# Attention for one query over a long cache: the wait for the output's landing moves behind the block's closing barrier

## The chip, the cores and the metric

The kernel runs on one core of a Trainium2 chip. The metric is the device time of one execution in microseconds; three runs of the kernel before gave 632.2, 632.3 and 632.31 us, median 632.3.

A core has five engines, each with its own instruction queue: TensorE (PE; its weight loads are listed as PEld), VectorE (DVE), ScalarE (ACT), GpSimd (POOL) and SyncE (SP). SyncE computes nothing here; it issues transfers, which sixteen DMA engines carry out. Engines and transfers wait for one another through semaphores: a transfer adds 16 to its semaphore when it has landed.

## The reference

The computation is attention with grouped queries: 32 query heads, 8 heads of K and V, one query position, 65,536 cached positions, 128 elements per head. Inputs and output are bf16.

```
B, Hq, Hkv, Sq, Sk, D = 1, 32, 8, 1, 65536, 128
k, v = repeat each head of k and v Hq // Hkv = 4 times
scores = einsum("bhqd,bhkd->bhqk", q, k) * D ** -0.5
p      = softmax(scores, axis=-1)
out    = einsum("bhqk,bhkd->bhqd", p, v)
```

K and V together are 268.4 MB and each byte is used once; the output is 8 KB.

## The kernel before

Each head's 65,536 positions are four chunks of 16,384, and two chunks make a pair, so there are 16 pairs. SyncE's function `sync_engine` issues all loads: for each pair two K transfers into `kbuf[0]` and `kbuf[1]` (4 MB each; cut into smaller pieces for the first and last pair) and V into `vbuf`. Before it reloads a buffer it waits for `kfree` or `vfree`, which the engines raise when they have read it.

For every chunk TensorE transposes K in tiles of 128 (line 116), VectorE and ScalarE copy the transposed tiles from PSUM to SBUF (lines 174 and 171), TensorE multiplies them with four queries (line 125), VectorE and GpSimd find the running maximum, ScalarE takes the exponentials and their sums, and TensorE multiplies with V (line 137). VectorE rescales and adds up the partial results. At the end of a head it divides by the sum (line 248, into `oT`).

Behind the loops stands a short tail, in which each step waits for the one before:

- `tensor_engine` waits for the last head (`t_o`) and transposes the result back (line 162).
- `vector_engine` rounds it to bf16 into `orow` (line 276) and raises `t_row`.
- `sync_engine` waits for `t_row`, issues the 8 KB output transfer (line 361), and waits for its landing on `o_sem` (line 362).

The five functions are the parts of one block (`nc.Block()`). Closing the block, which before happens in `es.close()` on line 370, sends every engine by a branch into a common closing barrier: each engine but GpSimd reports with a DRAIN that raises one semaphore, GpSimd waits for four reports and raises a second semaphore by four, and each of the others takes its release from it. All of these carry line 370 in the trace of before. A wait that stands directly ahead of an instruction is carried by it: before, SyncE's wait on `o_sem` is carried by SyncE's branch out of the block. A similar barrier opens the program (line 383).

`es.close()` then gives the semaphores and buffers back, which adds no instruction.

Of the kernel before, what the change touches and what calls it, by code (L numbers as in the profile page):

```python
# [29 lines left out]
def starts(sizes):  # L30
    return [sum(sizes[:i]) for i in range(len(sizes))]
# [8 lines left out]
def bass_standalone__gqa_softmax__decode_kernel(nc, q, k, v, out):  # L40
# [11 lines left out]
    S = es.enter_context  # L52
# [4 lines left out]
    def sem(name):  # L57
        return S(nc.semaphore(name))
# [43 lines left out]
    q_sem, o_sem, s_x, t_if, t_id, t_o, t_row = (  # L102
        sem(n) for n in ("q_sem", "o_sem", "s_x", "t_if", "t_id", "t_o", "t_row"))
# [219 lines left out]
    def sync_engine(e):  # L323
        W = T * D

        def src(x, p):
            h, c = p // 2, p % 2
            return x[h, c * 2 * P * T:(c + 1) * 2 * P * T, :].rearrange("(p t) d -> p (t d)", p=P)

        def pieces(to, s, sizes, sems):  # L330
            for a, w, sm in zip(starts(sizes), sizes, sems):
                e.dma_start(to[:, a * D:(a + w) * D], s[:, a * D:(a + w) * D]).then_inc(sm, 16)

        def tokens(sems):
            for sm in sems:
                e.sem_inc(sm, 16)

        for p in range(NP):
            ks, vs = src(kf, p), src(vf, p)
            for n in range(2):  # L340
                if p:
                    e.wait_ge(kfree[n], p)
                if p in (0, NP - 1):
                    pieces(kbuf[n], ks[:, n * W:(n + 1) * W], K_PIECES[n], kp[n])
                else:
                    e.dma_start(kbuf[n][:, :], ks[:, n * W:(n + 1) * W]).then_inc(kp[n][0], 16)
                    tokens(kp[n][1:])
            if p:
                e.wait_ge(vfree, p)
            if p in (0, NP - 2):  # L350
                for n in range(2):
                    e.dma_start(vbuf[:, n * W:(n + 1) * W], vs[:, n * W:(n + 1) * W]).then_inc(vp[n][0], 16)
                tokens(vp[1][1:])
            elif p < NP - 1:
                e.dma_start(vbuf[:, :], vs).then_inc(vp[0][0], 16)
                tokens(vp[1])
            else:
                for n in range(2):
                    pieces(vbuf[:, n * W:(n + 1) * W], vs[:, n * W:(n + 1) * W], V_PIECES[n], vp[n])
        e.wait_ge(t_row, 1)  # L360
        e.dma_start(of, orow[:, :]).then_inc(o_sem, 16)
        e.wait_ge(o_sem, 16)

    block = S(nc.Block())
    block.tensor(tensor_engine)
    block.vector(vector_engine)
    block.scalar(scalar_engine)
    block.gpsimd(gpsimd_engine)
    block.sync(sync_engine)
    es.close()  # L370

# [26 lines left out]
```

## Time and profile before

| | |
|---|---|
| median of three runs | 632.3 us (632.2 to 632.31) |
| profiled execution, its own time | 632.31 us |
| its span, first to last instruction | 630.5 us |
| time of that execution outside the span | 1.81 us |
| mean granted TensorE clock | 0.77 of full speed |
| moved | 268.59 MB, 426 GB/s over the span |

The span runs from the first to the last instruction of the program on any engine; the execution's own time is longer by what lies around it. In the views, a name with a q behind it (SPq, POOLq) is the engine's sequencer, which handles branches, semaphores, DRAINs and the issue of transfers; these aren't counted as busy time. "Us to landing" is the time from a transfer's issue to its semaphore. A row of a waits view names who waited, for whom, the total in us, how often and the longest. A row of the view of one line gives durations in ns (least, median, greatest) and the first and last start in us.

### The profile page before, as it was taken

To read this page: it belongs to the slowest core of one execution; us is meant where nothing else is said; L and a number is where in the kernel's file an instruction comes from. 1 tells how busy PE (TensorE), PEld (TensorE's weight loads), DVE (VectorE), ACT (ScalarE), POOL (GpSimd) and SP (SyncE) were. 2 spreads that over 40 slices of the span, in tenths; PEclk is the share of its full clock that TensorE was granted. 3 is DMA by queue.
4 is the path that set the end of the run, shared out by engine and by line. 5 is a ranking of instruction groups with operands and counts; after the bars stand their busy time and mean duration, and the time that the engine had idled before them with its cause. 6 is when DMAs were issued, how large, how long until landed. Compare 5 with 4: busy or idle time off the path is not lost. (4 is left out here: it accounts for less than half of the span.)

```text
span 630.5 us, 27839 instructions
## 1 busy us (share of the span) xinstructions
PE 485.2 (77%) x12290; PEld 479.9 (76%) x12290; DVE 316.8 (50%) x691; ACT 184.4 (29%) x411; POOL 16.0 (3%) x46
## 2 busy tenths in 40 slices
PE   6766859688696877958679585894968949689895
PEld 6766859687696877958679585894958849689894
DVE  5523717347173472825628165381644707447382
ACT  2321413314143140412504124041341413414241
POOL 0000000000000000000000000000000000000000
PEclk9877959779597795967959687595876958769595
DMA  8999999999999999999999999999999999999996
GB/s 357 438 429 446 437 412 453 412 453 424 420 445 420 445 422 431 453 414 451 414 432 447 418 447 418 432 451 414 451 414 451 428 418 447 420 430 432 417 436 260
DMA packets 9034, 268.59 MB, mean 426 GB/s; under 512 B 1088, under 2 KB 1088, under 8 KB 1856
## 3 DMA queue, kind: packets, MB, share of 16 engines
q1 hardware_dynamic: 8976, 268.45, 99.0%
q8 instruction: 6, 0.10, 0.1%
q14 instruction: 4, 0.03, 0.0%
q10 hardware_dynamic: 48, 0.01, 0.0%
HBM read 268.44 MB, written 0.01 MB: 426 GB/s over the span
## 5 line engine op out<-in xcount | busy, mean ns | idle before, releaser
L116 PE MATMUL trb<-ident,kbuf 128*128 128x128 bf16 x4096 | 335.9, 233 | 39.6 <-PEq L37 39.3
L174 DVE COPY ktb<-trb 128x1024 bf16<-128x1024 bf16 x384 | 255.1, 691 | 115.8 <-DVEq L37 115.0
L116 PEld LDWEIGHTS trb<-ident,kbuf 128*128 128x128 bf16 x4096 | 262.6, 104 | 41.0 <-issue 41.0
L171 ACT ACTIVATE ktb<-trb 128x1024 bf16<-128x1024 bf16 x128 | 131.1, 1024 | 386.5 <-ACTq L37 386.5
L125 PE MATMUL qkb<-qcur,ktb 128*128 128x4 bf16 x4096 | 175.2, 165 | 12.5 <-PEq L37 8.9
L137 PE MATMUL pvb<-pts,vbuf 128*128 128x4 bf16 x4096 | 112.3, 166 | 86.8 <-PEq L37 80.3
L137 PEld LDWEIGHTS pvb<-pts,vbuf 128*128 128x128 bf16 x4096 | 111.0, 104 | 88.1 <-issue 88.0
L125 PEld LDWEIGHTS qkb<-qcur,ktb 128*128 128x128 bf16 x4096 | 157.1, 97 | 14.8 <-issue 13.6
L286 ACT ACTIVATE pts<-qkb,negm 128x128 bf16<-128x128 f32 x128 | 50.7, 546 | 0.0
L212 DVE TENSOR_TENSOR acc<-acc,pvb 128x4 f32<-128x4 f32 x24 | 3.8, 158 | 85.3 <-DVEq L37 85.3
L286 ACT ACTIVATION_READ_ACCUMULATOR pts<-qkb,negm 128x1 f32 x128 | 35.4, 276 | 0.0
L183 DVE TENSOR_REDUCE cmax<-qkb 128x4 f32<-128x512 f32 x32 | 21.9, 686 | 21.5 <-DVEq L37 21.5
L210 DVE COPY acc<-pvb 128x4 f32<-128x4 f32 x8 | 1.3, 163 | 49.8 <-DVEq L37 49.8
L318 POOL PARTITION_ALL_REDUCE cmaxa<-cmax x32 | 11.9, 371 | 533.0 <-POOLq L37 533.0
L282 ACT ACTIVATE alpha<-dm 128x4 f32<-128x4 f32 x24 | 4.9, 202 | 46.2 <-ACTq L37 46.2
L193 DVE TENSOR_TENSOR m<-m,cmaxa 128x4 f32<-128x4 f32 x24 | 3.9, 163 | 8.0 <-DVEq L37 7.8
L202 DVE TENSOR_TENSOR acc<-acc,alpha 128x4 f32<-128x4 f32 x24 | 3.9, 163 | 6.6 <-DVEq L37 6.6
L203 DVE TENSOR_TENSOR lp<-lp,alpha 128x4 f32<-128x4 f32 x24 | 3.9, 163 | 3.7 <-DVEq L37 0.4
L204 DVE TENSOR_TENSOR lp<-lp,rsum 128x4 f32<-128x4 f32 x24 | 3.9, 163 | 3.5
L194 DVE TENSOR_TENSOR dm<-m 128x4 f32<-128x4 f32 x24 | 3.9, 162 | 3.5
L320 POOL PARTITION_ALL_REDUCE la<-lp x8 | 3.4, 430 | 72.7 <-POOLq L37 72.7
L195 DVE TENSOR_SCALAR negm<-m 128x4 f32<-128x4 f32 x24 | 3.9, 162 | 0.0
(32 smaller groups left out, 20.5 us busy)
## 6 DMA issues: line engine op xcount, KB each, us to landing
kbuf<-in_k_dram SPq DMA_DIRECT2D x28, 4096.0 KB, 26.7
vbuf<-in_v_dram SPq DMA_DIRECT2D x5, 4096.0 KB, 30.7
kbuf<-in_k_dram SPq DMA_DIRECT2D x6, 2048.0 KB, 21.6
kbuf<-in_k_dram SPq DMA_DIRECT2D x4, 512.0 KB, 11.9
kbuf<-in_k_dram SPq DMA_DIRECT2D x2, 1024.0 KB, 14.3
vbuf<-in_v_dram SPq DMA_DIRECT2D x1, 2048.0 KB, 29.6
vbuf<-in_v_dram SPq DMA_DIRECT2D x1, 1024.0 KB, 31.7
vbuf<-in_v_dram SPq DMA_DIRECT2D x2, 512.0 KB, 32.8
```

What stands on the lines that cost most here:

```text
L116: ins = pe.transpose(trb[j % NTB][:, i * P:(i + 1) * P], kv[:, t, :], ident[:, :])
L125: ins = pe.matmul(qkb[n][:, t * R:(t + 1) * R], lhsT=ktb[:, off:off + P], rhs=qcur[:, :], start=True, stop=True)
L137: ins = pe.matmul(pvb[n][:, 0:R], lhsT=vv[:, t, :], rhs=pts[n][:, t * R:(t + 1) * R], start=t == 0, stop=t == T - 1)
L171: e.activation(dst, trb[j % NTB][:, :], AF.Copy).then_inc(eva, 1)
L174: e.tensor_copy(dst, trb[j % NTB][:, :]).then_inc(evd, 1)
L183: e.tensor_reduce(cmax[:, :], qkb[n][:, :].rearrange("p (t g) -> p g t", g=R), AX.X, ALU.max).then_inc(cm, 1)
L193: own(e, e.tensor_tensor(mn[:, :], mo[:, :], cmaxa[:, :], ALU.max), xd)
L194: e.tensor_tensor(dm[:, :], mo[:, :], mn[:, :], ALU.subtract)
L195: e.tensor_scalar(negm[:, :], mn[:, :], -scale, None, ALU.mult).then_inc(ng, 1)
L282: e.activation(alpha[:, :], dm[:, :], AF.Exp, scale=scale)
L286: ins = e.activation(pv[:, g, :], sv[:, g, :], AF.Exp, bias=negm[:, g:g + 1], scale=scale, accum_out=rsum[:, g:g + 1])
L318: e.partition_all_reduce(cmaxa[:, :], cmax[:, :], P, bass.bass_isa.ReduceOp.max).then_inc(cma, 1)
```

## The change

The block is closed explicitly, and SyncE's wait on `o_sem` is issued behind it. SyncE now issues the output transfer, goes through the closing barrier with the other engines, and then waits for the transfer. The instructions of the other four engines stay the same and in the same order. On SyncE the branch no longer carries a wait, and one semaphore instruction is added as its last.

```
         e.wait_ge(t_row, 1)
         e.dma_start(of, orow[:, :]).then_inc(o_sem, 16)
-        e.wait_ge(o_sem, 16)
-
-    block = S(nc.Block())
-    block.tensor(tensor_engine)
-    block.vector(vector_engine)
-    block.scalar(scalar_engine)
-    block.gpsimd(gpsimd_engine)
-    block.sync(sync_engine)
+
+    with nc.Block() as block:
+        block.tensor(tensor_engine)
+        block.vector(vector_engine)
+        block.scalar(scalar_engine)
+        block.gpsimd(gpsimd_engine)
+        block.sync(sync_engine)
+    nc.sync.wait_ge(o_sem, 16)
     es.close()
```

## The prediction

> **What bounds the kernel now.** I began with the page's head and its strip of forty slices, to see which resource is full, and then cut the span at the points where the last stage changes its nature.
>
> ```profile
> span 630.5 us, 27839 instructions
> ...
> PE 485.2 (77%) x12290; PEld 479.9 (76%) x12290; DVE 316.8 (50%) x691; ACT 184.4 (29%) x411; POOL 16.0 (3%) x46
> ...
> DMA  8999999999999999999999999999999999999996
> ```
>
> ```profile
> core 0: us, PE busy (x) PEld busy (x) DVE busy (x) ACT busy (x) POOL busy (x), PEclk, DMA share, GB/s
> 0.72:626.50 625.78, 484.25 (x12273) 479.25 (x12273) 316.20 (x688) 184.42 (x411) 15.84 (x42) 0.77 1.00 429
> 626.50:628.71 2.21, 0.94 (x17) 0.61 (x17) 0.60 (x3) 0.00 (x0) 0.00 (x0) 0.50 0.00 0
> 628.71:630.11 1.40, 0.00 (x0) 0.00 (x0) 0.00 (x0) 0.00 (x0) 0.00 (x0) 0.50 0.03 6
> 630.11:630.50 0.39, 0.00 (x0) 0.00 (x0) 0.00 (x0) 0.00 (x0) 0.00 (x0) 0.50 0.00 0
> ```
>
> The page says that no engine is full (77% at most) and that the transfer engines are busy in nine tenths or more of nearly every slice. The table by windows sharpens it: for the first 626.5 us the DMA share is 1.00 at 429 GB/s. So the kernel is bound by loading K and V, and whatever sits beside that stream is free. Then come three short stages with no load in flight. The first, 2.21 us, finishes the arithmetic. The second, 1.40 us, has no engine busy and a DMA share of 0.03. The third, 0.39 us, has nothing busy at all. Only the last two can be touched by the change, so I read the timeline there, and then SyncE's own waits.
>
> ```profile
> 627.38 0.16 DVE L212 TENSOR_TENSOR acc<-acc,pvb 128x4 f32<-128x4 f32 x1 [4.29 <-DVEq L37]
> 627.69 0.16 DVE L248 TENSOR_TENSOR oT<-acc,recip 128x4 f32<-128x4 f32 x1
> 627.96 0.10 PEld L162 LDWEIGHTS qkb<-identf,oT 128*32 128x32 f32 x1 [0.82 <-issue]
> 627.99 0.37 PE L162 MATMUL qkb<-identf,oT 128*32 128x128 f32 x1 [0.76 <-DVE oT L248]
> 628.40 0.28 DVE L276 CAST orow<-qkb 32x128 bf16<-32x128 f32 x1 [0.56 <-PE qkb L162]
> 628.71 0.36 SPq L361 DMA_DIRECT2D out_dram<-orow  x1
> ```
>
> ```profile
> SPq L361 <- DVE orow L276: 34.9, 1, 34.9
> ...
> SPq L370 <- DMA out_dram<-orow: 1.0, 1, 1.0
> ...
> SPq L370 <- PEq L370: 0.2, 1, 0.2
> ```
>
> ```profile
> qsb<-in_q_dram ACTq DMA_DIRECT2D x1, 8.0 KB, 2.8
> out_dram<-orow SPq DMA_DIRECT2D x1, 8.0 KB, 1.4
> ```
>
> The timeline is a strict sequence: last sum, division, transposition back, rounding, and the issue of the output transfer at 628.71. SyncE has been waiting for that rounding for 34.9 us. The list of transfers gives 1.4 us from issue to landing: 628.71 + 1.4 = 630.1, and the waits agree, since SyncE's issue ends at 628.71 + 0.36 = 629.07 and it then waits 1.0 us for the landing. What follows the landing is in the view of line 370, where the block closes; the columns are engine queue, instruction, durations in ns, first and last start in us.
>
> ```profile
> L370 POOLq EVENT_SEMAPHORE  x2: 17/17/17, 630.3 to 630.4; - x2
> L370 ACTq DRAIN  x1: 8/8/8, 619.5 to 619.5; - x1
> L370 POOLq DRAIN  x1: 403/403/403, 622.3 to 622.3; - x1
> L370 PEldq DRAIN  x1: 415/415/415, 628.0 to 628.0; - x1
> L370 DVEq DRAIN  x1: 318/318/318, 628.4 to 628.4; - x1
> L370 SPq COMPARE_BRANCH  x1: 38/38/38, 630.1 to 630.1; - x1
> L370 SPq DRAIN  x1: 7/7/7, 630.3 to 630.3; - x1
> L370 SPq EVENT_SEMAPHORE  x1: 17/17/17, 630.4 to 630.4; - x1
> L370 ACTq EVENT_SEMAPHORE  x1: 17/17/17, 630.4 to 630.4; - x1
> L370 DVEq EVENT_SEMAPHORE  x1: 21/21/21, 630.4 to 630.4; - x1
> L370 PEldq EVENT_SEMAPHORE  x1: 51/51/51, 630.4 to 630.4; - x1
> ```
>
> This is the closing barrier. Each engine reports in with a DRAIN, GpSimd collects the reports and releases everyone with two semaphore instructions, and each engine takes its release. ACT has been there since 619.5, GpSimd since 622.3 + 0.4, the last of the others, DVE, since 628.4 + 0.3 = 628.7. SyncE alone is late: its branch out of the block carries the wait for the landing, runs at 630.1, reports at 630.3, and all are released at 630.4. The last instruction of the program is the release of TensorE, which ends the span at 630.5.
>
> **The change, part by part.** Nothing before 628.71 is touched: the loops, the loads and their semaphores are the same instructions in the same order on every engine. Two things differ on SyncE.
>
> First, the wait leaves the branch at the block's end. SyncE's branch can then run when the issue of the output is done, at 629.07, and no longer at 630.1. Behind the branch lie, by the rows of line 370, 0.2 us to SyncE's report, 0.1 us to GpSimd's release and 0.1 us until the last engine has taken it: 630.5 − 630.1 = 0.4 us, and by the window that runs from the landing to the end 0.39 us. In the new order this stretch runs from 629.07 to 629.5. The other engines are no obstacle, since the last of them reported at 628.7. So the whole barrier lies under the transfer, with 630.1 − 629.5 = 0.6 us to spare. The cover is the 1.0 us that remains of the flight after the issue; a transfer that landed 0.6 us sooner would still hide it, one that landed 1.0 us sooner would leave the 0.4 us bare, as now.
>
> What could make SyncE reach the barrier later than 629.07 is its own issue. Its length here is 0.36 us; the loads of line 332 bound it.
>
> ```profile
> L332 SPq DMA_DIRECT2D kbuf<-in_k_dram x12: 328/426/502, 0.7 to 580.4; - x12
> L332 SPq DMA_DIRECT2D vbuf<-in_v_dram x5: 327/432/438, 591.6 to 593.4; - x5
> ```
>
> At 502 ns it would be 0.14 us later, which the 0.6 us absorbs.
>
> Second, a wait for the landing is added behind the barrier, as an instruction of its own on SyncE. Before, it rode on the branch. Nothing is queued behind it on SyncE and no engine waits for SyncE after the barrier. Its price is its own execution after the landing: the semaphore instruction of SyncE in the rows above takes 17 ns, 0.02 us. Its bounds are that 0.02 us below and, above, the 0.2 us that passed between the branch's wake-up at 630.1 and SyncE's next instruction at 630.3, in case what delays that one is the wake-up and not the branch. I take the lower end, because the instruction is of the very kind of the 17 ns row, while the 0.2 us stand behind a branch.
>
> The sum: the end of the span moves from 630.5 to the landing plus the wait, 630.11 + 0.02 = 630.13; that is 0.37 us less. Around the span lie 632.31 − 630.5 = 1.81 us in the profiled execution, which no row of the trace resolves. I leave them as they are for the likeliest case, so 632.31 − 0.37 = 631.94 us. The profiled execution, 632.31, is that of the runs to 0.01 us (median 632.3), so the forecast is 631.9. That is 0.06% of the time. A difference within 0.2%, that is 1.26 us, is about what a measurement of this kernel can tell from no change; so I call this no change, with a small gain inside it.
>
> **The rivals.**
>
> The barrier isn't hidden, so that the change doesn't do what it says. The rows of line 370 speak for it in one way: a DRAIN does wait for its engine's unfinished work (415 ns on TensorE behind the transposition of 0.37 us, 318 ns on VectorE behind the rounding of 0.28 us, against 8 ns on ScalarE, which was idle). SyncE's DRAIN is 7 ns, but its transfer had landed by then, so no row shows a DRAIN of SyncE with a transfer in flight. If it waited for the landing, only the branch and its 0.2 us would go under the transfer: report at 630.1, release and taking of it 0.2 us, end at 630.3 and 632.1 in all. Against it: the DMA instruction itself ends on SyncE after 0.36 us, 1.0 us before landing, so for the engine's queue the work is done by then. If the unresolved 1.81 us are what counts and not SyncE's end, it stays at 632.3.
>
> The early release gains more than the barrier. Four engines are free at 629.5 in place of 630.5. If their work after the program is what fills the 1.81 us, it starts 1.0 us sooner: 629.5 + 1.81 = 631.3 us. It speaks for this that 1.81 us is a good deal of time for nothing; against it, that something must wait for SyncE, and SyncE is done only at 630.13, leaving 1.2 us for its part. This case is bounded by 1.0 us, 0.16%, and doesn't leave the band. The Trainium skill, on the page "Runtime: NRT & Kernel Launch", in the section "The ~15µs preamble/postamble breakdown", states that a barrier of about 1.5 us follows the kernel and waits for all engines, and elsewhere in the section that such a barrier walks the engines at 44 ns for each of 8 hops. By it the engines released early would wait there for SyncE and this rival could win at most the hops already walked, an estimate of 0.35 us, thus 631.6 in place of 631.3; no row here shows that part, and the page's sum of stages is larger than the 1.81 us that this case has outside the span.
>
> The landing becomes late, which is the way to a slower kernel. The four released engines do whatever they do after the program (the 1.81 us) while the output is still in flight, from 629.5 to 630.1; before, the transfer was alone, with a DMA share of 0.03. The list of transfers shows what the same 8 KB cost under traffic: the queries, issued at the start beside the first loads, took 2.8 us against 1.4. At that price the landing is at 631.5 and the time 631.94 + 1.4 = 633.3. It decides against the change from 0.37 us of delay on, and passes 0.2% from 0.37 + 1.26 = 1.63 us. Against it: the queries met several 512 KB loads, and nothing like that is issued behind the program in this trace; the window after the landing shows 0 GB/s. The skill's page "DMA: Bandwidth & Descriptors", section "Latency and other measured facts", puts the access to HBM at 0.2 us on average and 2 us at high load and makes it the larger part of a transfer's fixed cost. By that figure the rival would cost up to 1.8 us, an estimate, and give 633.7; by the trace, where the bus is empty at this place, the low end holds.
>
> **How the numbers follow.** Barrier hidden, outside unchanged, 631.9: 0.76. Barrier not hidden, 632.1 to 632.3: 0.10. Early release gains more, 631.3 to 631.9: 0.07. Late landing, 632.3 to 633.7: 0.04, of which half passes 0.2%. That leaves 0.03 for what no row shows, a load stream of 626 us that runs slightly differently in a newly built program, equally to both sides. The first three cases span 631.3 to 632.3; the runs before lie within 0.11 us (632.2 to 632.31), and some part of the late landing belongs into eight tenths, so the range is 631.2 to 632.7. Faster by over 0.2% needs 1.26 us, more than the 1.0 us of the second rival: 0.03, from the load stream and from an early release that saves more than the rows allow. Slower by over 0.2%: 0.04, half of the late landing and the load stream. Within: 0.93.
>
> **What would show it.** In the profile after, the view of the block's closing line should have SyncE's branch at about 629.1 and all releases at about 629.5, before the landing; a semaphore wait of SyncE alone should stand at 630.1 and be the last instruction; the span should be 630.1, and the first 626.5 us should be the same in DMA share and rate. A SyncE DRAIN of about 1 us instead of 7 ns would show the first rival; a time outside the span of clearly less than 1.81 us the second; a landing of over 1.8 us the third. The prediction is wrong if the load stage moves by a microsecond, or if the time outside the span grows by what the span loses.

## The result and the profile after

Twenty runs of the changed kernel gave 631.31 to 631.57 us, median 631.4; twenty of the kernel before, 632.13 to 632.43, median 632.3. The two sets don't overlap. The ratio is 0.9986, with a 95% interval of 0.998 to 0.9992: 0.9 us faster, 0.14%, inside the prediction's band of 0.2%. The forecast was 631.9, so the kernel gained 0.9 us where 0.4 us was predicted.

First the windows of the profile after, cut at the same places as before: at 0.72 and 626.50 us, at the issue of the output transfer, here 628.73, and at its landing.

```profile
0.72:626.50 625.78, 483.85 (x12273) 478.82 (x12273) 316.08 (x688) 184.44 (x411) 15.88 (x42) 0.77 1.00 429
626.50:628.73 2.23, 0.94 (x17) 0.61 (x17) 0.60 (x3) 0.00 (x0) 0.00 (x0) 0.50 0.00 0
628.73:630.11 1.38, 0.00 (x0) 0.00 (x0) 0.00 (x0) 0.00 (x0) 0.00 (x0) 0.50 0.03 6
```

The load stage has the same DMA share, 1.00, and the same 429 GB/s; the arithmetic tail is 2.23 us against 2.21. Nothing came from there. Next the line on which the block now closes, 363, and SyncE's wait behind it, line 369.

```profile
L363 POOLq EVENT_SEMAPHORE  x2: 17/17/17, 629.3 to 629.4; - x2
L363 ACTq DRAIN  x1: 8/8/8, 619.2 to 619.2; - x1
L363 POOLq DRAIN  x1: 404/404/404, 622.3 to 622.3; - x1
L363 PEldq DRAIN  x1: 415/415/415, 628.0 to 628.0; - x1
L363 DVEq DRAIN  x1: 318/318/318, 628.4 to 628.4; - x1
L363 SPq DRAIN  x1: 118/118/118, 629.1 to 629.1; - x1
L363 SPq EVENT_SEMAPHORE  x1: 17/17/17, 629.4 to 629.4; - x1
...
L363 PEldq EVENT_SEMAPHORE  x1: 51/51/51, 629.4 to 629.4; - x1
```

```profile
L369 SPq EVENT_SEMAPHORE  x1: 17/17/17, 630.1 to 630.1; - x1
```

```profile
SPq L369 <- DMA out_dram<-orow: 0.7, 1, 0.7
```

SyncE's DRAIN, its report to the barrier, starts at 629.1, everyone is released at 629.4, and SyncE alone is left: its waits show 0.7 us on the landing, until 630.1. The list of transfers still gives the output 1.4 us to landing. The span is 630.1 us against 630.5. So the part that the trace shows has the size that was forecast. The rest of the gain isn't in the trace: in the profiled executions the time outside the span is 631.48 − 630.1 = 1.4 us after, against 1.8 us before. Over the runs, each with its own span (given to 0.1 us), the mean outside is 1.33 us after (20 runs) and 1.81 us before (108 runs taken beside the experiments, in four groups of 1.80 to 1.81). The experiments ask where those 0.48 us went.

### The profile page after: what moved, and what is told of

Same layout as the page of the kernel before. It is cut to its first block, busy times and chain, and to the rows that moved or that the text cites. A ratio compares the mean times of both kernels' runs of the same rounds, so it can differ in the third digit from the quotient of the medians.

```text
span 630.1 us, 27839 instructions
## 1 busy us (share of the span) xinstructions
PE 484.8 (77%) x12290; PEld 479.4 (76%) x12290; DVE 316.7 (50%) x691; ACT 184.4 (29%) x411; POOL 16.1 (3%) x46
```

## The experiments

Every kernel of the experiments was run eleven times, beside runs of the kernel before, whose median lay between 632.25 and 632.30. The row of the changed kernel has the twenty runs from above; it wasn't run again beside the experiments. "Outside" is the mean over the runs of time less span. A ratio's interval is about 0.09% to either side, some 0.6 us, so what is compared below are medians and the ranges of the runs, which are a few tenths of a microsecond wide.

| kernel | median (range), us | ratio to before (95%) | outside, us |
|---|---|---|---|
| changed kernel (SyncE waits) | 631.40 (631.31–631.57) | 0.9986 (0.998–0.9992) | 1.33 |
| wait inside again | 632.29 (632.17–632.34) | 1.0 (0.9991–1.0009) | 1.80 |
| all five wait | 631.92 (631.78–632.16) | 0.9995 (0.9986–1.0004) | 1.82 |
| VectorE waits | 631.50 (631.45–631.68) | 0.9987 (0.9978–0.9996) | 1.45 |
| ScalarE waits | 631.54 (631.50–631.68) | 0.9989 (0.998–0.9998) | 1.47 |
| TensorE waits | 631.72 (631.59–631.93) | 0.9992 (0.9983–1.0001) | 1.62 |
| GpSimd waits | 631.94 (631.86–632.30) | 0.9995 (0.9986–1.0004) | 1.86 |
| all but SyncE wait | 632.02 (631.83–632.10) | 0.9996 (0.9987–1.0005) | 1.84 |
| SyncE sends and waits twice | 632.81 (632.70–632.91) | 1.0008 (0.9999–1.0017) | 1.31 |
| GpSimd later, 1 clear | 631.51 (631.41–631.61) | 0.9987 (0.9978–0.9996) | 1.40 |
| GpSimd later, 2 clears | 631.76 (631.64–631.87) | 0.9992 (0.9983–1.0001) | 1.64 |
| GpSimd later, 3 clears | 632.03 (631.89–632.14) | 0.9995 (0.9986–1.0004) | 1.90 |
| GpSimd later, 6 clears | 632.77 (632.73–632.94) | 1.0008 (0.9999–1.0017) | 1.90 |

### The place of the wait, or the new form of closing

My theory after the result was the prediction's second rival: four engines are released 1.0 us earlier, and work of theirs after the program, which no view shows, used to set the end. The rival was that a newly laid out program merely has another overhead. Two runs separate them. The first keeps the new form and puts the wait back.

```
         e.dma_start(of, orow[:, :]).then_inc(o_sem, 16)
+        e.wait_ge(o_sem, 16)
...
-    nc.sync.wait_ge(o_sem, 16)
```

> The block is closed explicitly as in the changed kernel, but SyncE's wait for the landing stands inside the block again, ahead of the barrier. It tells the place of the wait from the new form of closing the block. Theory A (what was gained comes from the order of landing and barrier: 0.4 us of barrier, and about 0.45 us outside the span because four engines are released early): this is the kernel before, 632.3 us, span 630.5, 1.8 us outside. Rival D (the 0.45 us outside the span come from the newly laid out program and not from the release): 631.8 to 631.9, span 630.5, 1.35 us outside.

Measured: 632.29 us, 1.80 us outside, as the kernel before. Its closing line shows the old order, with SyncE's branch at the landing and the report behind it.

```profile
L364 SPq COMPARE_BRANCH  x1: 38/38/38, 630.1 to 630.1; - x1
L364 SPq DRAIN  x1: 7/7/7, 630.3 to 630.3; - x1
```

The form alone is worth nothing. The second keeps the barrier hidden but lets nobody go early.

```
-    nc.sync.wait_ge(o_sem, 16)
+    for e in (nc.tensor, nc.vector, nc.scalar, nc.gpsimd, nc.sync):
+        e.wait_ge(o_sem, 16)
```

> Behind the closing barrier all five engines wait for the landing, not SyncE alone. The barrier stays hidden, but no engine is released early. Theory A: the span is that of the changed kernel, 630.1 us, but the time outside it goes back to 1.8 us, so 631.9, which was the forecast for the changed kernel. Rival D: 631.4 as the changed kernel, 1.35 us outside the span.

Measured: 631.92 us, 1.82 us outside. The view of the added line shows all five leaving together.

```profile
L370 SPq EVENT_SEMAPHORE  x1: 17/17/17, 630.0 to 630.0; - x1
L370 ACTq EVENT_SEMAPHORE  x1: 17/17/17, 630.0 to 630.0; - x1
L370 POOLq EVENT_SEMAPHORE  x1: 17/17/17, 630.0 to 630.0; - x1
L370 DVEq EVENT_SEMAPHORE  x1: 21/21/21, 630.0 to 630.0; - x1
L370 PEldq EVENT_SEMAPHORE  x1: 51/51/51, 630.0 to 630.0; - x1
```

This splits the gain: hiding the barrier is worth 632.3 − 631.92 = 0.4 us, and the early release of the others 631.92 − 631.40 = 0.5 us. The span is that of the changed kernel, 630.1 us, in both; the half microsecond lies wholly outside it.

### Which engine sets the end

Call an engine's closing part what has to be added to its last instruction to reach the end of the execution; any time that lies ahead of the first instruction is in this number, alike for every engine. Three forms of the theory were open: closing parts that run side by side (A1), a chain that walks the engines in order (A2), or parts that hinder one another when all start together (A3). In each of four runs another engine is the one that waits.

```
-    nc.sync.wait_ge(o_sem, 16)
+    nc.scalar.wait_ge(o_sem, 16)      # or nc.tensor, nc.vector, nc.gpsimd
```

> Behind the barrier ScalarE waits for the landing in place of SyncE; the other four are released at about 629.5. It asks how long each engine's own work after the program is. Theory A1 (each engine has a closing part of its own, they run side by side, and the time is that of the last; SyncE's is 1.35 us, and one other engine's is 1.8): 631.4 or less, unless ScalarE is the engine with 1.8 us, then 631.9. Theory A2 (the closing work is one chain that walks the engines in order, and an engine that comes late leaves only the steps behind it): a time between 631.1 and 632.0 that depends on ScalarE's place in the chain. Theory A3 (the closing parts hinder one another when all five start at once): 631.4, whichever engine it is.

> Behind the barrier TensorE waits for the landing in place of SyncE. Theory A1 (parallel closing parts): 631.4 or less, or 631.9 if TensorE is the engine whose part takes 1.8 us; its semaphore instruction is also the slowest, 51 ns against 17. Theory A2 (a chain in order): another time than with ScalarE, the two differing by the steps between them. Theory A3 (parts that hinder one another): 631.4 as with any engine.

> Behind the barrier VectorE waits for the landing in place of SyncE. So far the time outside the span is 1.34 us with SyncE last, 1.47 with ScalarE, 1.60 with TensorE and 1.83 with all five. Theory A1 (closing parts side by side, the longest sets the end): then VectorE or GpSimd has a part of 1.8 us, and with VectorE last the time is 631.9 if it is VectorE, under 631.9 if it is GpSimd. Theory A2 (a chain, each later engine cheaper): 1.2 to 1.75 us outside, below the 1.83 of all five, with VectorE as with GpSimd.

> Behind the barrier GpSimd waits for the landing in place of SyncE. Theory A1: 631.9 (1.8 us outside) if VectorE last stayed clearly below that, since one engine must have the 1.8 us. Theory A2: below 1.75 us outside here too, so that no single engine has the 1.83 us and the engines' closing parts add to one another.

Measured outside the span: VectorE 1.45, ScalarE 1.47, TensorE 1.62, GpSimd 1.86 us, beside SyncE's 1.33. The view of GpSimd's added wait has it at the landing, inside a span of 630.1 us:

```profile
L369 POOLq EVENT_SEMAPHORE  x1: 17/17/17, 630.0 to 630.0; - x1
```

The engines differ, so A3 falls. GpSimd alone costs as much as all five together (1.82), where A2 expected less than 1.75 from any single engine, so A2 falls in the form in which it was put down. What stands is the sum of A1: the time is the latest, over the engines, of last instruction plus closing part, and GpSimd has the longest part. That the parts run side by side isn't shown by this. A chain that takes GpSimd first, then TensorE, ScalarE, VectorE and SyncE, and waits at each step for that engine, costs a late engine its own step and all those behind it; it obeys the same sum and gives the same times in every run here. The complement, in which only SyncE goes early, agrees with the sum too:

```
-    nc.sync.wait_ge(o_sem, 16)
+    for e in (nc.tensor, nc.vector, nc.scalar, nc.gpsimd):
+        e.wait_ge(o_sem, 16)
```

> Behind the barrier the four engines other than SyncE wait for the landing, and SyncE is released at 629.5. Theory A1 (side by side): the longest part is among these four, so 631.9 with 1.8 us outside, as with all five. Theory A2 (a chain that takes something from every engine that is late): less than 1.83 us by SyncE's share and more than the dearest single engine, 1.65 to 1.8 us.

Measured: 632.02 us, 1.84 us outside, within the scatter of all five.

### Is SyncE's part a constant?

```
     nc.sync.wait_ge(o_sem, 16)
+    nc.sync.dma_start(of, orow[:, :]).then_inc(o_sem, 16)
+    nc.sync.wait_ge(o_sem, 32)
```

> SyncE waits behind the barrier as in the changed kernel, then sends the same output a second time and waits for that too; the other four engines are released at about 629.5 as there. It makes SyncE later still against the others, by one flight of 1.4 us. Theory A1 and A2 (what SyncE has left to do after its last wait is the same once the others are out of its way): the span grows by 1.4 us to 631.5 and the time outside it stays 1.33 us, so 632.8. If more could still be hidden, the time outside would shrink further, below 1.3; if the others' work had not been done at 630.1, it would shrink here and the time be below 632.7.

Measured: 632.81 us, 1.31 us outside; the last wait moved to 631.5, one flight later.

```profile
L371 SPq EVENT_SEMAPHORE  x1: 17/17/17, 631.5 to 631.5; - x1
```

Giving the other engines 1.4 us more lead takes nothing further off. In the changed kernel SyncE's own end is already what counts, and the 1.4 us by which the last landing came later are all in the time.

### Making GpSimd late on purpose

The sum of A1 says that the time is the latest of the engines' ends, each with its own closing part, whoever executes the last instruction of the program. Rival B was that the closing work starts at the last instruction and is only dearer when that is GpSimd's. Here GpSimd, done with the barrier at 629.3 to 629.4, is kept for a while with a small tile, and SyncE waits as in the changed kernel.

```
     nc.sync.wait_ge(o_sem, 16)
+    for _ in range(1):      # 1, 2, 3 or 6
+        own(nc.gpsimd, nc.gpsimd.memset(lw[:, :], 0.0), xg)
```

> The changed kernel, in which GpSimd, once released by the barrier at about 629.4, clears a small tile that nobody reads any more and waits for that, once; SyncE waits for the landing at 630.1 as before. It makes GpSimd later by about 0.2 us without making it the last. Theory A1 (the time is the latest of all engines' ends, each with its own closing part: 1.34 us for SyncE, about 1.85 for GpSimd): GpSimd would be done at 629.6 + 1.85 = 631.45, SyncE at 631.4, so the time is still 631.4 to 631.5. Rival B (the closing work starts with the last instruction of the program, and costs 0.5 us more only when that is GpSimd's): 631.4.

> As the one before with three such clears and waits, so that GpSimd is done at about 629.95, still ahead of SyncE's wait, which ends the span at 630.1. Theory A1: 629.95 + 1.85 = 631.8, although the span is that of the changed kernel. Rival B: 631.4, since SyncE is still the last.

> As the one before with six, so that GpSimd is done at about 630.5, after SyncE. Both theories: about 630.5 + 1.85 = 632.35, and 1.85 us outside a span that now ends with GpSimd.

GpSimd's last instruction is its last semaphore wait of line 37; the row of the view of that line ends its range at 629.5 us with one clear, 630.1 with three and 630.9 with six.

```profile
L37 POOLq EVENT_SEMAPHORE  x43: 17/17/17, 0.9 to 629.5; - x43
```

```profile
L37 POOLq EVENT_SEMAPHORE  x45: 17/17/17, 0.9 to 630.1; - x45
```

```profile
L37 POOLq EVENT_SEMAPHORE  x48: 17/17/17, 0.9 to 630.9; - x48
```

Measured: 631.51, 632.03 and 632.77 us, which are 630.1 + 1.9 and 630.9 + 1.9 in the last two. With three clears the run missed its purpose: a clear with its wait took longer than I had counted on, GpSimd was done together with SyncE, and both theories give the same. With one clear A1 had 631.4 to 631.5 and B 631.4; 631.51 leans to A1 but is no proof. The clears themselves cost nothing outside the span, since three and six of them both show 1.90 us there. So the case between was run.

> The changed kernel with two clears and waits on GpSimd behind the barrier. A clear with its wait took 0.255 us in the runs with one, three and six of them, more than the 0.2 us counted on, so with three GpSimd ended together with SyncE's wait and the two theories gave the same. With two it is done at about 629.8, some 0.3 us ahead of SyncE. Theory A1 (latest of the engines' ends, each with its own closing part, GpSimd's 1.85 to 1.9 us): 631.65 to 631.75, 1.6 us outside an unchanged span of 630.1. Rival B (only the engine of the last instruction counts): 631.4 and 1.33 us outside.

Measured: 631.76 us, 1.64 us outside. GpSimd's last wait and SyncE's, in the views of lines 37 and 369:

```profile
L37 POOLq EVENT_SEMAPHORE  x44: 17/17/17, 0.9 to 629.9; - x44
```

```profile
L369 SPq EVENT_SEMAPHORE  x1: 17/17/17, 630.2 to 630.2; - x1
```

GpSimd is done 0.3 us before SyncE, and still the time grew by 0.36 us over the changed kernel, in a span that differs by no more than the runs' scatter. Each of its eleven runs has 1.6 us or more outside the span, and none of the changed kernel's twenty over 1.4. The execution that these rows show took 631.87 us: GpSimd's 629.9 + 1.9 = 631.8 comes to it, SyncE's 630.2 + 1.33 = 631.5 doesn't. B falls.

## Why the prediction was right or wrong

**The load stage is untouched: right.** DMA share 1.00 and 429 GB/s in both profiles, the tail 2.23 against 2.21 us.

**The barrier goes under the flight: right, in its place and size.** The prediction had SyncE's branch at 629.07, its report 0.2 us behind that, and the barrier done at 629.5. The DRAIN starts at 629.1 and takes 0.12 us, and the last release starts at 629.4. What fills the stretch differs: the branch of 38 ns, with the 0.2 us behind it, isn't in the trace any more, and the DRAIN takes 118 ns where it took 7. That the two come to about the same length is luck; the prediction had carried the branch over.

**The added wait costs its own execution: right.** It is 17 ns at 630.1, and the span shrank from 630.5 to 630.1. The kernel in which all five engines wait isolates this step and the one before: 631.92 us, where the prediction's sum said 631.94.

**The time around the span stays 1.81 us: wrong, and this is the step that failed.** It was carried over because no row resolved it. It is 1.33 us after, and the runs show why. Each engine has a closing part after its last instruction, the latest end is the time, and GpSimd's part is the longest: 1.85 to 1.9 us, against 1.33 us for SyncE. Before, GpSimd's last instruction in the barrier stood at 630.4, and 630.4 + 1.9 = 632.3 is the measured time. The change moves it to 629.4, so that GpSimd is done at 629.4 + 1.9 = 631.3, and SyncE, at 630.1 + 1.33 = 631.4, is now the last. So 0.9 us of the 1.0 us by which GpSimd leaves earlier reach the result; then SyncE caps it.

**The rivals.** The second one happened, in the bounded form in which it stood: no later than 631.9, no sooner than 631.3, with the objection that something must wait for SyncE. Its sign, named in advance, was a time outside the span of clearly less than 1.81 us. That 631.4 lies inside the range is owed to this rival's lower end of 631.3 and not to the sum, which gave 631.94. It had 0.07 of the chance, which was too little: no row of the trace favoured an unchanged 1.81 us over it. The rows didn't show which of the four engines matters; the experiments show that holding GpSimd alone until the landing undoes the whole of it, 1.86 us outside. An identical 1.81 us behind a barrier that changes who leaves when is an assumption and not a reading. The prediction worked out from the Trainium skill's page "Runtime: NRT & Kernel Launch", section "The ~15µs preamble/postamble breakdown", that this rival could win at most an estimated 0.35 us; measured are 0.5 us, between all five waiting and SyncE alone. The same section also lists clearing of 51 semaphores on each engine behind the kernel, which could be a part that each engine does for itself; no run here shows what the closing parts consist of. The first rival fell on the DRAIN: 118 ns, and not the 1.0 us of the flight. The third fell on the landing, which stayed at 1.4 us with four engines already in their closing parts.

**What stays open.** What the closing parts are, whether they run side by side or as a chain that begins with GpSimd, and why GpSimd's is 0.5 us longer than SyncE's, the trace doesn't show. It wasn't tried to leave out the wait for the landing altogether, since the program could then end with its output in flight. Of the five engines that can wait, SyncE is the cheapest, by 0.1 us over VectorE, whose runs overlap with SyncE's; none of these kernels is faster than the changed one.

## What to carry to other kernels

The time of an execution is more than the span: in this kernel each engine has a closing part behind its last instruction, and the latest of these ends is the result. So let every engine that has nothing left to do leave early, GpSimd above all, and let the engine that waits for the last landing be SyncE, behind the closing barrier; one kernel was measured, so measure it again in yours. When a change alters which engine is released when, don't carry the time outside the span over unchanged; bound it from the engine that left last and the one that will.

## What the runs showed of the hardware that was not expected

- The time outside the span depends on the engine that ends last: 1.33 us for SyncE, 1.45 for VectorE, 1.47 for ScalarE, 1.62 for TensorE, 1.86 for GpSimd. All five together cost 1.82, no more than GpSimd alone.
- An engine that is not the last can set the time: with GpSimd done at 629.9 and SyncE at 630.2, the time followed GpSimd; the median was 631.76 us against 631.40 in the changed kernel.
- SyncE's DRAIN right behind the issue of a transfer took 118 ns, against 7 ns when the transfer had landed; it doesn't wait for the landing, which came 0.9 us after it.
